# One block's first products moved from plain float32 to three split passes, with reordered first transfers and pinned weight decoding

## The chip, the cores and the metric

The kernel runs on one core of a Trainium2 chip. The metric is device time in microseconds (us) of the whole program: the median of a few executions. A profile of one execution is shown beside it; its span runs from the first instruction to the last, and the execution's own time is a little longer than its span.

## What is computed

Three layers follow each other, all in float32 (shapes in brackets):

```python
# attention: 4 batches, 8 heads, 768 positions, 64 wide; chunks of 32 queries
# see 16 positions to the left, 8 to the right and 8 memory slots
scores = 0.125 * q_c @ k_full.T; a = softmax(scores); out = a @ v_full
x = out as [3072 tokens, 512]
h = x @ w_in                    # [512, 2048]
x = (h * cos(h)) @ w_out        # [2048, 512]
h = max(x @ w1, x @ w2, x @ w3) # each [512, 768]
y = h @ w2o                     # [768, 512]
```

## The kernel before, in words

**Two ways to multiply.** A float32 product on TensorE is made either "plain", one matmul instruction on float32 operands (which the trace shows as two records), or "split": each operand is held as a high part (rounded to the fp32r type by ScalarE, called ACT) and a low part (what the rounding left over, a subtraction on VectorE or GpSimd, called DVE and POOL), and three matmuls, high by high, high by low and low by high, are added up in PSUM. `products` does either, according to how many parts of the moving operand it is given. The low part of a weight must be there before the third matmul of a product.

**Blocks and slots.** The 3072 tokens are 8 blocks of 384 columns, numbered 0 to 7. The first feed-forward layer has 16 feature tiles `f`. A slot is one (block, feature tile): `p1` makes h = w_in[f]ᵀ x (4 products over 512 inputs), `chain` makes g = h cos(h) on ACT and DVE, and `p2`, two slots later (`LOOK`), adds w_out[f]ᵀ g into 4 accumulators (4 products). A tile h lies in one of two PSUM buffers, so the `p1` two slots on needs the `chain` of this one to be done. In block 0 both `p1` and `p2` are plain; from block 1 on both are split. Blocks 6 and 7 are cut into halves of 8 feature tiles, run in the order 6, 7, 6, 7, so that the second layer's weights find room; from block 7's first half (`turn`) on, `p2` comes three slots later (`LOOKB`). When a new block's `p2` begins, the four accumulators must have been copied out by ACT and DVE (L392, L394).

**Attention** of block 0 runs ahead of everything, as a loop of 9 steps (scores at step i, normalizing at i-1, transposing at i-2, values at i-3), each third of it needing its own q, k and v. Later blocks' attention is spread over the slots by tables (`FIRST` for block 0: S scores, E exponentials, N normalizing, T transposing, V values).

**Weights** arrive as 512 KB tiles (`raw`) and must be decoded: a cast makes the top half (`w_top`, on POOL L162 or ACT L160, into one of two `top` buffers in turn), and a shift-and-or on DVE joins both halves (`w_bits`, L177); splitting them is `w_split` (L185 on ACT, then L186 on DVE or POOL). `keysA` lists w_in and w_out tiles alternately, `keysB` the second layer's 24 tiles. `Decode` hands this work out slot by slot, at the places `fill` in `chain`; a scheduler may move these instructions. In block 0 decoded tiles of both kinds are kept plain and split later.

**The second layer** (`b3`, `b4`) runs 48 steps of 36 and 9 matmuls; the last three `p2` stand behind its first `b3`.

All transfers of this kernel are issued by SyncE (SP), in order. `LOADS` is the order of the first ones: q0 is q and k of the first third of block 0, v0 its values, w the next weight tile. By the page's sizes a q is 256 KB (of 1024 bytes), a k 320, a v 384 and a weight tile 512.

Of the kernel before, what the change touches and what calls it, by code (L numbers as in the profile page):

```python
# [32 lines left out]
N = 384  # L33
# [19 lines left out]
FIRST = {0: "S0", 1: "S1", 2: "S2", 3: "E", 5: "N0", 6: "N1 T0", 7: "V0", 9: "T1", 10: "V1", 11: "N2", 12: "T2", 13: "V2"}  # L53
# [6 lines left out]
LOADS = "q0 q1 w q2 v0 v2 w w w w v1 w"  # L60
WARM0, WARM = 11, 2
PRO = (0, 0, 0, 0, 0, 1, 0, 1, 0)
PROL = (1, 2, 0, 2, 2, 3, 0, 3, 2)
PROE = (0, 2, 2, 3, 0, 2, 1, 0, 2)
# [4 lines left out]
RATE, RATEB, AHEADB = 2, 0.75, 4  # L69
# [3 lines left out]
SPLIT0, SPLITS = 5, (1, 1.5)  # L73
# [4 lines left out]
def attn_moe_kernel(ctx, tc, qT, kT, vw, w_in, w_out, w3, w2o, out):  # L78
    nc = tc.nc
    PE, ACT, DVE, POOL, SP = nc.tensor, nc.scalar, nc.vector, nc.gpsimd, nc.sync  # L80

# [73 lines left out]
    def w_top(key, eng):  # L155
        raw = wst[key].rearrange("p c t -> p (c t)").bitcast(BF16).rearrange("p (c t) -> p c t", t=4)[:, :, 2]
        top[key] = tops[len(top) % NTOP]
        o = top[key].bitcast(F16).rearrange("p (c t) -> p c t", t=2)[:, :, 1]
        if eng is ACT:
            ACT.activation(out=o, in_=raw, func=AF.Copy)  # L160
        else:
            eng.tensor_copy(o, raw)  # L162
# [3 lines left out]
    def w_bits(key):  # L166

        z = o = wst[key][:, :, 0]
        if key in numA:
            i, odd = divmod(numA[key], 2)  # L170
            if not odd:
                plain[i] = (wp if i < FA - 1 else tmp["pool"]).tile([128, 2, 512], I32, tag="w", name="wt")
                live[0] += i < FA - 1
# [3 lines left out]
        DVE.scalar_tensor_tensor(o, z, 13, top[key], op0=ALU.logical_shift_right, op1=ALU.bitwise_or)  # L177
        wst[key] = o.bitcast(F32)

    def w_split(key, eng):  # L180
# [4 lines left out]
        ACT.activation(out=w[:, 0, :], in_=c, func=AF.Copy)  # L185
        eng.tensor_tensor(w[:, 1, :], c, w[:, 0, :].bitcast(F32), op=ALU.subtract)  # L186
        n = numA.get(key, -1)
        live[0] -= n % 2 if n < 2 * FA - 1 else 0
# [80 lines left out]
    def a_v(d, ts=(0, 1), pool=None):  # L269
# [3 lines left out]
        if o == 0 and ts[0] == 0:  # L273
            xT[j] = xp.tile([128, 2, 4, N], F32R if j else F32, tag="x", name="x")
# [10 lines left out]
        if j:  # L285
            DVE.tensor_tensor(x[:, 1, :, sl], s[:, :, c0:c1], x[:, 0, :, sl].bitcast(F32), op=ALU.subtract)
# [48 lines left out]
    def p1(j, f, ps):  # L335
# [5 lines left out]
        for k in range(4):  # L341
            products(h, w, k, [x[:, i, k, :] for i in range(2 if j else 1)], k == 0, k == 3)
# [3 lines left out]
    def g_tile(dtype=F32R):  # L346
        p = tmp["pool"] if done[0] else gp
        return p.tile([128, 2, N], dtype, tag="g", name="g", bufs=4 if done[0] else 3)

    def chain(j, f, fill):  # L350
# [135 lines left out]
    class Decode:  # L486


        def __init__(self, keys, exp_eng, lo_eng):
            self.keys, self.exp_eng, self.lo_eng = keys, exp_eng, lo_eng  # L490
            self.nl = self.ne = self.nb = self.ns = 0
# [8 lines left out]
        def room(self):  # L500
            if self.keys is keysB:
                return self.nl - self.ns < AHEADB and live[0] + 3 <= NW
            return self.nl - self.nb < 9 and live[0] + 3 <= NW

        def exp(self, upto):
            while self.ne < min(self.nl, upto, self.nb - len(self.ops) + NTOP):
# [3 lines left out]
        def begin(self, n):  # L510
            keys = self.keys[self.nb:min(self.nb + n, self.nl)]
# [37 lines left out]
    for i in range(2 * DB + 3):  # L549
# [26 lines left out]
    def slot(s):  # L576
# [5 lines left out]
        ready = dec.nb if dec.keys is keysB else 0  # L582
        calm = s < turn or all(slots[s - i][0] == slots[s - i + 1][0] for i in (LOOKB, LOOKB - 1))
        if dec.keys is keysA:
            dec.begin(RATE)
        elif calm:
            dec.begin(max(0, min(2, int(RATEB * (s - turn)) - dec.nb)))
# [137 lines left out]
```

## Time and profile before

| what | us |
|---|---|
| median of three runs | 1080.37 (1078.62 to 1081.43) |
| profiled execution, own time | 1080.69 |
| its span | 1078.8 |
| TensorE (PE) busy | 1059.4 |
| DVE, ACT, POOL busy | 467.4, 434.8, 267.1 |

How to read it: TensorE's busy time is 98% of the span, and in the other 19.4 us it stands still. A matmul counts as busy at whatever clock it is granted, so busy time holds stretches at half clock too. The other engines' idle time costs nothing by itself.

### The profile page before, as it was taken

Reading aid. Unit: us, or ns where it says so; the run is one execution under the profiler, and the core shown is the slowest. Engines: PE = TensorE matmul, PEld = TensorE weight load, DVE = VectorE, ACT = ScalarE, POOL = GpSimd, SP = SyncE. Lnnn points to the kernel's source line nnn. Section 1 sums busy time; section 2 is a strip of 40 time slices with the busy share of each in tenths; the row PEclk is TensorE's granted clock in tenths of the full one; section 3 lists DMA queues with packets and bytes.
Section 4 is the critical chain, followed back from the end, with each engine's and each line's share of the span. In section 5 each row is a group of like instructions: output and inputs, shape, how many; then the busy total and the mean of one; then the engine's idle time right before and its main releaser. Section 6 shows DMA issues by size and latency. Waiting matters only on the chain.

```text
span 1078.8 us, 16695 instructions
## 1 busy us (share of the span) xinstructions
PE 1059.4 (98%) x6861; PEld 978.5 (91%) x6861; DVE 467.4 (43%) x856; ACT 434.8 (40%) x797; POOL 267.1 (25%) x240
## 2 busy tenths in 40 slices
PE   7999999999999999999999999999999999999998
PEld 5565699999999999999999899999999999999997
DVE  5689465555455454544537656222222122312221
ACT  4577455545455454454537657111112121211111
POOL 1356243423233233233313346010101010110000
PEclk8899999999999999999999999999999999999999
DMA  9970121111111111210116525110101020100000
GB/s 319 276 291 17 37 74 52 60 52 52 38 52 52 60 44 38 67 37 16 45 55 196 166 92 167 44 30 30 30 30 30 30 79 10 59 1 31 1 30 30
DMA packets 29837, 76.05 MB, mean 70 GB/s; under 512 B 3392, under 2 KB 8512, under 8 KB 29760
## 3 DMA queue, kind: packets, MB, share of 16 engines
q1 hardware_dynamic: 29760, 74.97, 21.2%
q8 instruction: 54, 0.88, 0.3%
q14 instruction: 23, 0.19, 0.1%
HBM read 60.80 MB, written 14.16 MB: 69 GB/s over the span
## 4 chain that ended last, share of the span: by engine, by line
PE 84%; DMA 5%; DVE 5%; ACT 4%; issue 2%; POOL 0%; SPq 0%; ACTq 0%; DVEq 0%; POOLq 0%
PE h L439 28%; PE h L333 19%; PE acc L333 19%; PE acc L460 9%; PE s L224 3%; PE s L280 2%; PE s L263 2%; PE h L330 1%; DMA v<-in_vw_dram 1%; DMA raw<-in_w2o_dram 1%; PE acc L330 1%; DMA raw<-in_w_dram 1%; DVE w L186 1%; DVE wt L177 1%; DMA raw<-in_w_out_dram 1%
## 5 line engine op out<-in xcount | busy, mean ns | idle before, releaser
L439 PE MATMUL h<-x,w 128*128 128x384 f32 x1728 | 308.5, 335 | 2.2 <-DVE ki L372 2.2
L439 PEld LDWEIGHTS h<-x,w 128*128 128x128 f32 x1728 | 302.0, 188 | 6.5 <-DVE ki L372 2.5
L333 PE MATMUL acc<-g,w 128*128 128x384 f32 x1344 | 257.2, 338 | 2.2 <-ACT x L392 2.2
L333 PE MATMUL h<-x,w 128*128 128x384 f32 x1344 | 255.2, 337 | 0.0
L333 PEld LDWEIGHTS h<-x,w 128*128 128x128 f32 x1344 | 234.8, 188 | 2.9 <-ACT x L284 0.2
L333 PEld LDWEIGHTS acc<-g,w 128*128 128x128 f32 x1344 | 233.0, 188 | 4.1 <-ACT x L392 2.6
L375 POOL TENSOR_TENSOR g<-ki,g 128x384 fp32r<-128x384 f32 x112 | 115.8, 1034 | 274.8 <-ACT g L374 242.4
L367 DVE SCALAR_TENSOR_TENSOR ki<-h,ki 128x384 f32<-128x384 f32 x112 | 62.2, 555 | 144.2 <-ACT ki L365 144.0
L446 DVE TENSOR_TENSOR r<-h,r 128x384 f32<-128x384 f32 x48 | 26.8, 558 | 197.8 <-PE h L439 196.8
L460 PE MATMUL acc<-w,g 128*128 128x512 f32 x432 | 107.3, 393 | 0.0
L421 POOL TENSOR_TENSOR x<-xs,x 128x384 fp32r<-128x384 f32 x31 | 32.6, 1082 | 273.3 <-ACT x L420 273.3
L365 ACT ACTIVATE ki<-h 128x384 int32<-128x384 f32 x112 | 54.2, 484 | 107.0 <-PE h L333 105.6
L370 ACT ACTIVATE ki<-ki,pio 128x384 f32<-128x384 f32 x112 | 68.8, 614 | 68.1 <-DVE ki L368 67.9
L449 ACT ACTIVATE g<-r 128x384 fp32r<-128x384 f32 x48 | 25.1, 523 | 174.5 <-DVE r L447 174.5
L460 PEld LDWEIGHTS acc<-w,g 128*128 128x128 f32 x432 | 80.4, 188 | 14.7
L372 DVE TENSOR_TENSOR ki<-h,ki 128x384 f32<-128x384 f32 x112 | 62.3, 556 | 57.6 <-ACT ki L370 57.2
L374 ACT ACTIVATE g<-ki 128x384 fp32r<-128x384 f32 x112 | 58.5, 522 | 52.7 <-DVE ki L372 52.1
L445 ACT ACTIVATE r<-h 128x384 f32<-128x384 f32 x48 | 23.6, 492 | 130.1 <-PE h L439 130.1
L447 DVE TENSOR_TENSOR r<-h,r 128x384 f32<-128x384 f32 x48 | 26.8, 558 | 66.5 <-PE h L439 66.3
L368 DVE TENSOR_SCALAR ki<-ki 128x384 f32<-128x384 f32 x112 | 51.5, 459 | 3.1
L330 PE MATMUL h<-x,wt 128*128 128x384 f32 x128 | 47.1, 511 | 2.4 <-DVE g L362 1.9
L254 POOL TENSOR_TENSOR sm<-sm,rs 128x768 f32<-128x768 f32 x21 | 30.8, 1471 | 58.4 <-PE h L333 40.8
(80 smaller groups left out, 858.1 us busy)
## 6 DMA issues: line engine op xcount, KB each, us to landing
v<-in_vw_dram SPq DMA_DIRECT2D x24, 384.0 KB, 3.3
raw<-in_w_dram SPq DMA_DIRECT2D x18, 511.8 KB, 3.7
raw<-in_w_in_dram SPq DMA_DIRECT2D x16, 511.8 KB, 9.2
raw<-in_w_out_dram SPq DMA_DIRECT2D x16, 511.8 KB, 9.7
k<-in_kT_dram SPq DMA_DIRECT2D x24, 320.0 KB, 3.7
x2d<-x SPq DMA_DIRECT2D x40, 192.0 KB, 1.9
xs<-x2d SPq DMA_DIRECT2D x20, 384.0 KB, 3.2
q<-in_qT_dram SPq DMA_DIRECT2D x24, 256.0 KB, 2.7
```

Source lines behind the costliest of these rows:

```text
L330: PE.matmul(o, lhsT=w[:, sl], rhs=x[0], start=first, stop=last)
L333: PE.matmul(o, lhsT=w[a][:, sl], rhs=x[b], start=first and n == 0, stop=last and n == 2)
L365: ACT.activation(out=ki, in_=h, func=AF.Copy, scale=INV2PI, bias=0.25)
L367: DVE.scalar_tensor_tensor(c, h, INV2PI, ki, op0=ALU.mult, op1=ALU.subtract)
L368: DVE.tensor_scalar(c, c, -0.75, 0.25, op0=ALU.max, op1=ALU.min)
L370: ACT.activation(out=c, in_=c, func=AF.Sin, scale=2 * math.pi, bias=pio2)
L372: DVE.tensor_tensor(c, h, c, op=ALU.mult)
L374: ACT.activation(out=g[:, 0, :], in_=c, func=AF.Copy)
L375: POOL.tensor_tensor(g[:, 1, :], c, g[:, 0, :].bitcast(F32), op=ALU.subtract)
L421: (DVE if j == 0 and k == 3 else POOL).tensor_tensor(x[:, 1, k, :], t[:, i, :], x[:, 0, k, :].bitcast(F32), op=ALU.subtract)
L439: PE.matmul(h, lhsT=w[a][:, 128 * k:128 * k + 128], rhs=x[:, b, k, :], start=(n == 0), stop=(n == 11))
L460: PE.matmul(o[m], lhsT=g[:, a, 128 * m:128 * m + 128], rhs=w[b], start=(f == 0 and n == 0), stop=(f == FB - 1 and n == 2))
```

## The change

`p1` of block 0 becomes split, so the low half of block 0's x is made too, and each w_in tile is split as soon as it is decoded, always on POOL (`split_in`); only w_out tiles stay plain in block 0, and these are split at half a tile per slot from slot 5 on, at one per slot from slot 16 on (`split_out`, alternately DVE and POOL). v0 and v1 are loaded ahead of all weights. `keep` pins the instructions of decoding and splitting in the order of the program. Block 0's tables place the scores a slot later. For the second layer's weights (`keysB`), up to 6 tiles (4 before) may be loaded and unsplit, a tile is cast only once the slot after its load has come (`there`), decoding starts a slot later, and 3 instead of 2 tiles are taken per step after the slots. `p2` waits one more slot where a block begins, g has 5 buffers instead of 4 there, and one leftover `p2` stands between the second and third product group of the first `b3`.

```diff
-LOADS = "q0 q1 w q2 v0 v2 w w w w v1 w"
+LOADS = "q0 q1 v0 q2 v1 w w v2 w w w w"
...
-RATE, RATEB, AHEADB = 2, 0.75, 4
+RATE, RATEB, AHEADB = 2, 0.75, 6
...
-SPLIT0, SPLITS = 5, (1, 1.5)
+SPLIT0, SPLITS = 5, (0.5, 1)
...
+    keep = tc.keep_in_program_order
...
-        if key in numA:
-            i, odd = divmod(numA[key], 2)
+        if key[0] == "out":
+            i, odd = divmod(key[1], 2)
...
-        DVE.scalar_tensor_tensor(o, z, 13, top[key], op0=ALU.logical_shift_right, op1=ALU.bitwise_or)
+        keep(DVE.scalar_tensor_tensor(o, z, 13, top[key], op0=ALU.logical_shift_right, op1=ALU.bitwise_or))
...
-        if j:
-            DVE.tensor_tensor(x[:, 1, :, sl], s[:, :, c0:c1], x[:, 0, :, sl].bitcast(F32), op=ALU.subtract)
+        DVE.tensor_tensor(x[:, 1, :, sl], s[:, :, c0:c1], x[:, 0, :, sl].bitcast(F32), op=ALU.subtract)
...
-            products(h, w, k, [x[:, i, k, :] for i in range(2 if j else 1)], k == 0, k == 3)
+            products(h, w, k, [x[:, i, k, :] for i in range(2)], k == 0, k == 3)
...
             fill("d0")
+            fill("a0")
             ACT.activation(out=c, in_=c, func=AF.Sin, scale=math.pi)
             ACT.activation(out=c, in_=c, func=AF.Square)
-            fill("a0")
+            fill("a1")
...
         for e in range(3):
+            if e == 2 and n2[0] < total:
+                p2(*slots[n2[0]])
+                n2[0] += 1
...
+        def split_in(self, upto):
+
+            for k in self.keys[self.ni:upto]:
+                if k[0] == "in":
+                    w_split(k, POOL)
+            self.ni = max(self.ni, upto)
+
+        def split_out(self, upto):
+            while self.ns < min(upto, FA):
+                w_split(("out", self.ns), POOL if self.ns % 2 else DVE)
                 self.ns += 1
...
-        ready = dec.nb if dec.keys is keysB else 0
+        ready, dec.there, dec.soon = dec.nb, dec.soon, dec.nl
...
-            while n2[0] <= s - (LOOKB if s >= turn else LOOK):
+            last = s - LOOK
+            if s >= turn:
+                last = s - LOOKB - (slots[s - LOOKB][0] != slots[s - LOOKB - 1][0])
+            while n2[0] <= last:
```

The change shows in the order of instructions at three places. The first is SP's queue at the start of the program, before:

```order
L208 DMA q<-in_qT_dram 128x512
L209 DMA k<-in_kT_dram 128x640
L208 DMA q<-in_qT_dram 128x512
L209 DMA k<-in_kT_dram 128x640
L150 DMA raw<-in_w_in_dram 128x2047
L208 DMA q<-in_qT_dram 128x512
L209 DMA k<-in_kT_dram 128x640
L217 DMA v<-in_vw_dram 96x1024 x2
L150 DMA raw<-in_w_in_dram 128x2047
L150 DMA raw<-in_w_out_dram 128x2047
L150 DMA raw<-in_w_in_dram 128x2047
L150 DMA raw<-in_w_out_dram 128x2047
```

and with the change:

```order
L209 DMA q<-in_qT_dram 128x512
L210 DMA k<-in_kT_dram 128x640
L209 DMA q<-in_qT_dram 128x512
L210 DMA k<-in_kT_dram 128x640
L218 DMA v<-in_vw_dram 96x1024
L209 DMA q<-in_qT_dram 128x512
L210 DMA k<-in_kT_dram 128x640
L218 DMA v<-in_vw_dram 96x1024
L152 DMA raw<-in_w_in_dram 128x2047 x2
L218 DMA v<-in_vw_dram 96x1024
L152 DMA raw<-in_w_out_dram 128x2047
```

v0 has moved ahead of q2, v1 from behind five weight tiles to ahead of all of them, and the first weight tile from behind q1 to behind v1.

The second place is the first product of block 0. On DVE (px is the transposed attention weights, L177 or L179 a decode into raw or wt, L286 a low half of x, L356 the first DVE step of slot 0's chain) stands before:

```order
L318 TENSOR_TENSOR sm<-sm,rs 128x384
L267 COPY px<-s 96x512
L316 TENSOR_SCALAR rs<-rs 128x4
L317 RECIPROCAL rs<-rs 128x4
L177 SCALAR_TENSOR_TENSOR wt<-raw,top_85 128x512
L318 TENSOR_TENSOR sm<-sm,rs 128x384
L177 SCALAR_TENSOR_TENSOR wt<-raw,top_86 128x512
L267 COPY px<-s 96x512
L177 SCALAR_TENSOR_TENSOR wt<-raw,top_85 128x512
L356 SCALAR_TENSOR_TENSOR ki<-h,ki 128x384
```

and with the change:

```order
L316 TENSOR_SCALAR rs<-rs 128x4
L286 TENSOR_TENSOR x<-s,x 128x4x64
L179 SCALAR_TENSOR_TENSOR raw<-raw,top_86 128x512
L317 RECIPROCAL rs<-rs 128x4
L286 TENSOR_TENSOR x<-s,x 128x4x64
L318 TENSOR_TENSOR sm<-sm,rs 128x384
L286 TENSOR_TENSOR x<-s,x 128x4x64
L268 COPY px<-s 96x512
L179 SCALAR_TENSOR_TENSOR wt<-raw,top_85 128x512
L179 SCALAR_TENSOR_TENSOR raw<-raw,top_86 128x512
L286 TENSOR_TENSOR x<-s,x 128x4x64
L179 SCALAR_TENSOR_TENSOR wt<-raw,top_85 128x512
```

The low halves of x have come in between, and two decodes now stand behind the last px copy and ahead of the last low half. On TensorE (s<-k,q are the scores of block 1's first third, L224 or L225) stands before:

```order
L280 MATMUL s<-px,v 64x64 x8
L330 MATMUL h<-x,wt 128x384 x5
L224 MATMUL s<-k,q 64x96 x16
L330 MATMUL h<-x,wt 128x384 x5
L224 MATMUL s<-k,q 64x96 x16
L330 MATMUL h<-x,wt 128x384 x2
L330 MATMUL acc_565<-g,wt 128x384
L330 MATMUL acc_566<-g,wt 128x384
```

and with the change:

```order
L281 MATMUL s<-px,v 64x64 x8
L333 MATMUL h<-x,w 128x384 x24
L225 MATMUL s<-k,q 64x96 x16
L333 MATMUL h<-x,w 128x384 x12
L330 MATMUL acc_593<-g,wt 128x384
L330 MATMUL acc_594<-g,wt 128x384
L330 MATMUL acc_595<-g,wt 128x384
L330 MATMUL acc_596<-g,wt 128x384
L225 MATMUL s<-k,q 64x96 x16
L333 MATMUL h<-x,w 128x384 x12
```

The scores have moved from inside slot 1's products to behind them, so that slot 2's products come right behind the first scores.

The third place is TensorE's order where the second layer begins (h<-x,w at L439 or L443), before:

```order
L333 MATMUL acc_6214<-g,w 128x384 x3
L439 MATMUL h<-x,w 128x384 x36
L333 MATMUL acc_6211<-g,w 128x384 x3
L333 MATMUL acc_6212<-g,w 128x384 x3
L333 MATMUL acc_6213<-g,w 128x384 x3
L333 MATMUL acc_6214<-g,w 128x384 x3
L333 MATMUL acc_6211<-g,w 128x384 x3
```

and with the change:

```order
L333 MATMUL acc_6371<-g,w 128x384 x3
L443 MATMUL h<-x,w 128x384 x24
L333 MATMUL acc_6368<-g,w 128x384 x3
L333 MATMUL acc_6369<-g,w 128x384 x3
L333 MATMUL acc_6370<-g,w 128x384 x3
L333 MATMUL acc_6371<-g,w 128x384 x3
L443 MATMUL h<-x,w 128x384 x12
L333 MATMUL acc_6368<-g,w 128x384 x3
```

One leftover `p2` has moved from behind the third group of 12 matmuls to ahead of it.

## Rows read from the trace of the kernel before

**Rows 1.** The page: busy time; granted TensorE clock in 40 slices, in tenths.

```profile
PE 1059.4 (98%) x6861; PEld 978.5 (91%) x6861; DVE 467.4 (43%) x856; ACT 434.8 (40%) x797; POOL 267.1 (25%) x240
...
PEclk8899999999999999999999999999999999999999
```

**Rows 2.** Chain that ended last, 0 to 135 us: start, us, what.

```profile
30.63 5.71 PE h L330 x10
...
114.37 2.58 PE h L330 x8
...
124.69 2.09 PE h L333 x12
```

**Rows 3.** TensorE's waits: line, releaser, us in all, times, longest.

```profile
PE h L330 <- DVE g L362: 1.9, 2, 1.6
```

**Rows 4.** Timeline 14 to 40 us: start, us, engine, instruction, [idle before].

```profile
14.51 0.77 POOL L162 CAST top<-raw 128x512 f16<-128x512 bf16 x1 [5.53 <-DMA raw<-in_w_in_dram]
...
22.45 1.12 PE L280 MATMUL s<-px,v 96*64 96x64 f32 x16 [4.63 <-DMA v<-in_vw_dram]
...
30.19 0.38 ACT L284 ACTIVATE x<-s 128x256 f32<-128x256 f32 x1 [2.62 <-PE s L280]
...
37.33 1.09 DVE L236 TENSOR_TENSOR sm<-s,maskb 128x384 f32<-128x384 f32 x2
...
38.45 0.95 DVE L241 TENSOR_REDUCE mx<-sm 128x8 f32<-128x768 f32 x1
...
39.32 0.54 DVE L362 SCALAR_TENSOR_TENSOR g<-ki,h 128x384 f32<-128x384 f32 x1
```

**Rows 5.** Four stretches: us, busy us (instructions) by engine, clock, DMA share, GB/s.

```profile
22.45:30.63 8.18, 6.83 (x75) 5.28 (x75) 2.45 (x4) 2.12 (x5) 1.52 (x2) 0.50 1.04 338
30.63:36.34 5.71, 5.71 (x12) 2.97 (x14) 0.09 (x1) 0.59 (x2) 0.00 (x0) 0.61 1.04 266
106.00:108.00 2.00, 0.39 (x2) 0.30 (x2) 0.61 (x2) 1.97 (x5) 0.38 (x1) 1.00 0.00 0
612.00:614.00 2.00, 2.00 (x8) 2.00 (x7) 1.30 (x2) 1.96 (x4) 1.38 (x2) 0.50 0.81 290
```

**Rows 6.** Groups by form, 40 to 92 us: count, busy us, mean ns, idle.

```profile
L177 DVE SCALAR_TENSOR_TENSOR wt<-raw,top 128x512 int32<-128x512 int32 x28 | 26.6, 978 | 2.0 <-POOL top L162 1.3 <-ACT top L160 0.7
...
L162 POOL CAST top<-raw 128x512 f16<-128x512 bf16 x13 | 11.6, 894 | 12.0 <-DVE wt L177 11.2 <-DMA raw<-in_w_out_dram 0.8
...
L186 POOL TENSOR_TENSOR w<-wt,w 128x512 fp32r<-128x512 f32 x6 | 8.7, 1445 | 7.7 <-ACT w L185 7.7
...
L246 ACT ACT_TABLE_LOAD x2 | 2.6, 1283 | 0.0
```

**Rows 7.** Timeline 92 to 108 us: DVE and POOL making low halves.

```profile
92.65 4.29 DVE L186 TENSOR_TENSOR w<-wt,w 128x512 fp32r<-128x512 f32 x3
...
93.22 4.87 POOL L186 TENSOR_TENSOR w<-wt,w 128x512 fp32r<-128x512 f32 x3 [0.18 <-ACT w L185]
...
107.62 1.27 POOL L186 TENSOR_TENSOR w<-wt,w 128x512 fp32r<-128x512 f32 x1 [2.72 <-DVE g L362]
```

**Rows 8.** Timeline 608 to 671 us: the two late waits of TensorE.

```profile
608.49 0.78 ACT L160 ACTIVATE top<-raw 128x512 f16<-128x512 bf16 x1 [0.88 <-DMA raw<-in_w2o_dram]
...
609.91 0.86 ACT L392 ACTIVATE x<-acc 128x384 f32<-128x384 f32 x2
...
610.44 3.21 PE L333 MATMUL acc<-g,w 128*128 128x384 f32 x12 [2.24 <-ACT x L392]
...
616.43 2.24 PE L333 MATMUL acc<-g,w 128*128 128x384 f32 x12
...
670.81 2.37 PE L439 MATMUL h<-x,w 128*128 128x384 f32 x12 [2.21 <-DVE ki L372]
```

**Rows 9.** The page's transfers of w1 to w3, to landing; and the chain.

```profile
raw<-in_w_dram SPq DMA_DIRECT2D x18, 511.8 KB, 3.7
...
693.98 6.26 PE h L439 x36
```

More of the change, by code (lines that the diff above doesn't have):

```diff
@@ L159, in w_top @@
         if eng is ACT:
-            ACT.activation(out=o, in_=raw, func=AF.Copy)
+            keep(ACT.activation(out=o, in_=raw, func=AF.Copy))
         else:
-            eng.tensor_copy(o, raw)
+            keep(eng.tensor_copy(o, raw))
     plain = {}
@@ L184, in w_split @@
         assert live[0] <= NW
[L185 to L188, printed above, removed]
+        keep(ACT.activation(out=w[:, 0, :], in_=c, func=AF.Copy))
+        keep(eng.tensor_tensor(w[:, 1, :], c, w[:, 0, :].bitcast(F32), op=ALU.subtract))
+        live[0] -= key[0] != "out" or key[1] % 2 and key[1] < FA - 1
         DST[key[0]][key[1]] = (w[:, 0, :], w[:, 1, :])
@@ L273, in a_v @@
         if o == 0 and ts[0] == 0:
-            xT[j] = xp.tile([128, 2, 4, N], F32R if j else F32, tag="x", name="x")
+            xT[j] = xp.tile([128, 2, 4, N], F32R, tag="x", name="x")
         x = xT[j]
@@ L347, in g_tile @@
         p = tmp["pool"] if done[0] else gp
-        return p.tile([128, 2, N], dtype, tag="g", name="g", bufs=4 if done[0] else 3)
+        return p.tile([128, 2, N], dtype, tag="g", name="g", bufs=5 if done[0] else 3)
     def chain(j, f, fill):
@@ L501, in room @@
             if self.keys is keysB:
-                return self.nl - self.ns < AHEADB and live[0] + 3 <= NW
+                return self.nl - self.ns < AHEADB and live[0] + 5 <= NW
             return self.nl - self.nb < 9 and live[0] + 3 <= NW
         def exp(self, upto):
-            while self.ne < min(self.nl, upto, self.nb - len(self.ops) + NTOP):
+            while self.ne < min(self.there if self.keys is keysB else self.nl, upto, self.nb - len(self.ops) + NTOP):
                 w_top(self.keys[self.ne], self.exp_eng(self.ne))
@@ L510, in begin @@
         def begin(self, n):
-            keys = self.keys[self.nb:min(self.nb + n, self.nl)]
+            keys = self.keys[self.nb:min(self.nb + n, self.there if self.keys is keysB else self.nl)]
             self.nb += len(keys)
@@ L580, in slot @@
         base = DB * (j + 1)
-        ready = dec.nb if dec.keys is keysB else 0
-        calm = s < turn or all(slots[s - i][0] == slots[s - i + 1][0] for i in (LOOKB, LOOKB - 1))
+        ready, dec.there, dec.soon = dec.nb, dec.soon, dec.nl
+        calm = s < turn or s < total - 3 and all(slots[s - i][0] == slots[s - i + 1][0] for i in (LOOKB, LOOKB - 1))
         if dec.keys is keysA:
@@ L595, in fill @@
                 if where == "a0":
-                    dec.split(min(parts, len(keysA)))
+                    dec.split_in(ready)
+                elif where == "a1":
+                    dec.split_out(parts)
             elif where in ("a0", "a1"):
@@ L600, in fill @@
                 dec.bits(1)
-            elif where == "z" and calm:
-                dec.bits()
+            elif where == "z":
+                if calm:
+                    dec.bits()
+                    dec.exp(dec.nb + 2)
                 dec.load()
-                dec.exp(dec.nb + 2)
         p1(j, f, ps)
@@ L658, in attn_moe_kernel @@
         if n == 0:
-            for s in range(n2[0], total):
-                p2(*slots[s])
+            while n2[0] < total:
+                p2(*slots[n2[0]])
+                n2[0] += 1
         if n >= LOOK:
```

25 lines of the change are left out of this document (14 added, 11 removed).

## The prediction

> **What bounds the kernel now.** I read the page first. TensorE is busy for 98% of the span, and the clock row reads 9 (90% or more) but for slices at the start, where it reads 8 [rows 1]: so only three things are worth time, fewer TensorE cycles, less waiting of TensorE, and its clock.
>
> Fewer cycles: the chain of waits gives the price of the two kinds of product. In block 0's steady part four plain products (8 records) take 2.58 us, and block 1's first four split products (12 matmuls) 2.09 [rows 2].
>
> Waiting: TensorE's list of waits and the timeline name four places. It waits 4.63 us for v1, which sits behind five weight tiles in SP's queue [rows 4]; 1.9 us in two waits for the last step of a chain in block 0 (L362) [rows 3]; 2.24 us at 610 for ACT to empty an accumulator (L392), which ACT does late; and 2.21 us at 668 for a PSUM tile of the last chain [rows 8]. 1.3 us at the start and some 5 us at the end are of no concern here.
>
> Clock: the windows view shows the level. After the v1 wait it is 0.50 (1.2 GHz) all the way to the first product, and 0.61 on average over the first ten records, which take 5.71 us [rows 2, 5]. After the wait at 610 it reads 0.50 too, but after the one of about 1.6 us that ends at 107.66 the window reads 1.00 [rows 3, 5].
>
> **The change part by part.** I sum against the profiled execution's own time, 1080.69, which is 0.3 above the median.
>
> *Passes.* 16 `p1` of block 0 become split: 16 x (2.58 - 2.09) = **-7.8 us** at full clock. All block 0's other TensorE work stays. A lower bound is 0, if another engine then sets the pace (a rival below); more is excluded, as nothing else in block 0 loses cycles.
>
> *Prologue.* Six transfers then stand ahead of the last v instead of the weights. In today's trace the second weight tile, which closes the first 3.60 MB in the queue, has landed by 14.51 [rows 4]; with the change the same first 3.60 MB (by the sizes in the section on the kernel) hold three q and k, v0, v1 and two weight tiles, so v1, at 2.56 MB, is there well before TensorE asks for it at 22.45 - 4.63 = 17.82. From 22.45 to the first product at 30.63 are 8.18 us, of which TensorE is busy 6.83 at half clock [rows 2, 5]; at full clock that is 3.4 less, so the product could start at 17.82 + 8.18 - 3.4 = 22.6. New work stands ahead of it on DVE: six low halves of x, for which the nearest row is ACT's copy of the same half block, 0.38 [rows 4], and four decodes; their mean of 0.98 [rows 6] holds many that ran beside busy POOL work, and I take 0.7, since POOL has little to do yet. That is 6 x 0.38 + 4 x 0.7 = 5.1 us. DVE has room for about 1.5 of it while TensorE works; the last decode also waits for a POOL cast that queues behind the first weight's low half (0.9 and 1.27 [rows 6, 7]), which runs beside the px copies. I take 3.6 as exposed: start at 26.2, a gain of **-4.4 us**. Bounds: 22.6 (-8.0) to 30.6 (0). The first five plain products took 5.71 us and at 2.58 per four would take 3.2: with no long wait ahead of them the clock stays, **-2.5 us** (bounds -2.5 to 0).
>
> *A wait that comes in return.* Block 1's first scores move behind slot 1's products. DVE then has two additions (1.09) and a maximum (0.95) between them and slot 0's g (0.54) [rows 4], and slot 2's `p1` needs slot 0's PSUM tile. Today the scores run early, in the middle of slot 1. TensorE now reaches slot 2 as the scores end, the first addition begins half way through them, and so 0.55 + 0.95 + 0.54 = 2.0 us of DVE stand between. Slot 3 inherits a little: ACT has an exponential between the two chains with a table load on either side (1.28 each [rows 6]; in block 0 there are seven loads now, five before), and I put 0.8. Together **+2.8 us**; 0 if DVE gets to g earlier, 5 if the later two thirds cost as much.
>
> The table load is a place to weigh a rule. Rows 6 give 1.283 us for one, and in the timeline the ACTIVATE behind it starts at once. The Trainium skill ("ScalarE: Activation LUTs", What ACT_TABLE_LOAD costs) counts 2.66 us for a switch, a drain included; by that the two new ones would hold ACT 2.8 us longer, and the sum would be about 17 instead of 20 us. The trace does not agree, and no term uses it.
>
> *The rest of block 0.* The two waits of 1.9 us stand where the low halves of weights pile up on DVE and POOL: three on each take 4.29 and 4.87 us there, against 1.27 for a lone one on POOL [rows 3, 7]. Pinned and spread, none piles up: **-1.9 us** (0 to -1.9). ACT's extra roundings, 16 in block 0 instead of about half as many, and POOL's extra subtractions lie beside TensorE's 4.67 us a slot (2.58 + 2.09). If that cover is gone, the second rival tells.
>
> *The turn.* At 610 the new block's `p2` comes a slot later, so one more `p1` (2.09) lies over ACT's copy, and ACT is no longer held by casts of tiles that have not landed (0.88 at 608). The wait of 2.24 goes, and with it the half clock after it: from 610.44 to 616.43 are 5.99 us for two groups of 2.09, so 1.8 more. **-4.0 us** (bounds: 0 to -4.0). At 668, a `p2` of 2.09 fills the 2.21: **-2.1 us** (0 to -2.2) [rows 8].
>
> *Second layer.* Ten or so weight tiles are decoded in its first steps that were decoded before it. The 36 matmuls of a step alone take 6.3 us and the tiles fall due from the fifth step on, after 25 us or more, while a transfer lands in 3.7 us [rows 9] and up to six are in flight: **0**, with its price in the third rival.
>
> Sum: -7.8 - 4.4 - 2.5 + 2.8 - 1.9 - 4.0 - 2.1 = **-19.9**, so 1080.7 - 19.9 = 1060.8.
>
> **The rivals.**
>
> *First: the clock falls at the start.* Between 17.8 and 26 TensorE has only 3.4 us of this work in 8.4, with gaps that I estimate at 1 us each, and then the 2.0 us of the new wait. For it: after 2.24 us at 610 the clock fell [rows 5, 8]. Against it: after 1.6 us at 106 it did not. Half clock over the first two slots would give back the 2.5 and about 2 more: 1065.
>
> *Second: DVE and POOL set block 0's pace.* All w_in low halves go to POOL, beside DVE's decodes. For it: a decode takes 0.98 on average between 40 and 92 us, and POOL's low half 1.45 there against 1.27 alone [rows 6, 7]. Against it: in the pile-up three of each, made in 4.87 us, overlapped in part, and DVE loses about half of its own low halves. Counting a slot from rows 4 and 6, DVE has two decodes (2.0), the chain's two steps (2 x 0.54) and attention (an estimate: three times 1.09 + 0.95, and as much again for what follows, over 16 slots, 0.8): 3.9 us in a slot of 4.67, which is near. If the slot stayed at today's 2 x 2.58 = 5.16 from slot 4 on, 12 x 0.49 = 5.9 would be lost: 1066.7. At the worst POOL's 2.7 (a cast 0.9, a low half 1.45, a quarter of one more for w_out) would come wholly on top of DVE's 3.9, a slot would take 6.6, and 12 x 1.4 = 17 more would be lost: 1084. Most of that is excluded, since today's POOL has 1.6 a slot beside the same DVE work and TensorE waits for neither until 99 us. The Trainium skill ("GPSIMD Engine Reference", the specification table) says that POOL's way to SBUF is shared with VectorE and contended by instructions with two SBUF inputs, as decodes and low halves are; the lengthened rows agree that it is shared, the pile-up that it is not one at a time.
>
> *Third, on the other side: late weights of the second layer.* Were the ten late tiles fetched and converted one by one, each would take 3.7 + 0.9 (cast) + 1.0 (decode) + 1.45 (low half) = 7.0 us, 70 in all, against some 25 until they fall due: 45 us of waiting, 1106. It decides where fewer than three tiles are on the way at once; with six there is no wait. For it: ACT waits for landings today, 0.88 us of one at 608 [rows 8]. Against it: SP has nothing else to do then.
>
> *Fourth: better than said*, with the prologue at its bound and no new wait: 1055.
>
> **How the numbers follow.** Forecast (1057 to 1063) 0.45; first rival (1062 to 1067) 0.17; second (1063 to 1076) 0.2; fourth (1053 to 1057) 0.1; third (over 1084) 0.04; gains that cancel for reasons I don't see (1077 to 1084) 0.04. From 1054 to 1069 hold 0.8 of it. A measurement of this kernel tells about 0.3% (3.2 us) from no change; so faster 0.93, same 0.03, slower 0.04.
>
> **What would show it.** Right: TensorE's wait for v gone and its first split product near 26; a wait of about 2 us for L363 near 31; windows of 20 to 40 us at clock 1.00; no waits from 50 to 130; block 0's slots 0.49 shorter; no wait for L393 near 590; the first `b3` without a gap. Wrong: the windows at 0.50 near 30; many short waits of TensorE for DVE or POOL between 50 and 110; waits for raw tiles beyond 650. The prediction fails most easily in block 0, where one engine more in the pace undoes the passes.

## The result, and the profile after

The changed kernel takes 1064.99 us (median of 4 runs, 1064.47 to 1066.60); the kernel before took 1079.49 beside it (4 runs). The ratio is 0.9872, 95% interval 0.9843 to 0.9902: faster by 1.3%. The profiled execution's own time is 1064.75, its span 1062.5. The forecast was 1060.8, with 1054 to 1069 as its range; 1065 is where the first rival stood.

First the page after, its first group and its clock row, against [rows 1]:

```profile
PE 1048.6 (99%) x6925; PEld 986.2 (93%) x6925; DVE 460.0 (43%) x854; ACT 437.7 (41%) x799; POOL 281.0 (26%) x248
...
PEclk9899999999999999999999999999999999999999
```

Then TensorE's timeline around the first products (start, us, engine, instruction, idle before), which answers to [rows 2, 4]:

```profile
25.69 0.45 PE L333 MATMUL h<-x,w 128*128 128x384 f32 x1 [0.48 <-ACT x L285]
27.85 5.62 PE L333 MATMUL h<-x,w 128*128 128x384 f32 x23 [1.72 <-DVE x L286]
33.41 1.54 PE L225 MATMUL s<-k,q 64*64 64x96 f32 x32
37.05 3.75 PE L333 MATMUL h<-x,w 128*128 128x384 f32 x12 [2.11 <-DVE g L363]
...
40.60 2.96 PE L330 MATMUL acc<-g,wt 128*128 128x384 f32 x8
43.49 1.54 PE L225 MATMUL s<-k,q 64*64 64x96 f32 x32
45.49 2.35 PE L333 MATMUL h<-x,w 128*128 128x384 f32 x12 [0.46 <-DVE g L363]
47.68 2.74 PE L330 MATMUL acc<-g,wt 128*128 128x384 f32 x8
```

The wait of 4.63 us for v1 is gone. In its place stand 1.72 for the last low half of x and 2.11 for slot 0's g. Twelve split matmuls take 3.75 us at 37.05 and 2.35 at 45.49: the first group has less clock, as these windows show (columns as in rows 5):

```profile
26.00:28.00 2.00, 0.28 (x2) 0.15 (x1) 1.80 (x2) 0.00 (x0) 2.00 (x3) 0.85 1.03 390
28.00:30.00 2.00, 2.00 (x7) 2.00 (x8) 1.14 (x1) 0.00 (x0) 0.76 (x2) 0.50 1.09 271
...
36.00:38.00 2.00, 0.95 (x4) 0.95 (x5) 2.00 (x4) 1.02 (x1) 1.75 (x2) 0.91 1.04 246
38.00:40.00 2.00, 2.00 (x8) 2.00 (x8) 2.00 (x3) 1.53 (x2) 0.09 (x1) 0.50 1.01 356
```

The clock falls to 0.50 (1.2 GHz) twice, each time after a stretch in which TensorE was mostly idle. From 50 us on nothing of this is left, and the late stretch of [rows 8] has no wait either:

```profile
70.00:90.00 20.00, 20.00 (x143) 15.37 (x142) 12.54 (x21) 14.18 (x28) 11.46 (x9) 1.00 0.27 93
...
600.00:660.00 60.00, 60.00 (x349) 60.00 (x348) 35.86 (x56) 35.06 (x67) 28.33 (x26) 1.00 0.36 123
```

In slots without attention, two groups (p1 and p2) take 4.66 us from one `p1` to the next, as 2.09 + 2.58 said:

```profile
105.00 2.54 PE L333 MATMUL h<-x,w 128*128 128x384 f32 x12
...
109.66 2.54 PE L333 MATMUL h<-x,w 128*128 128x384 f32 x12
```

The same mark in both programs tells where the gain came. At the turn (the first pair of `p1`, 24 matmuls of L333) and at the second layer's first `b4`, the timelines of TensorE before read

```profile
562.28 4.32 PE L333 MATMUL h<-x,w 128*128 128x384 f32 x24
...
691.74 2.24 PE L460 MATMUL acc<-w,g 128*128 128x512 f32 x9
```

and after

```profile
552.70 4.32 PE L333 MATMUL h<-x,w 128*128 128x384 f32 x24
...
675.42 2.24 PE L464 MATMUL acc<-w,g 128*128 128x512 f32 x9
```

That is 9.6 us by the turn, where the terms up to there made 13.8, and 16.3 by the first `b4`, so 6.7 from the turn on, where the terms made 6.1.

### The profile page after: what moved, and what is told of

Read it like the earlier page. It is cut to its first block, busy times and chain, and to the rows that moved or that the text cites. A ratio compares the mean times of both kernels' runs of the same rounds, so it can differ in the third digit from the quotient of the medians.

```text
span 1062.5 us, 16809 instructions
## 1 busy us (share of the span) xinstructions
PE 1048.6 (99%) x6925; PEld 986.2 (93%) x6925; DVE 460.0 (43%) x854; ACT 437.7 (41%) x799; POOL 281.0 (26%) x248
## 4 chain that ended last, share of the span: by engine, by line
PE 98%; ACT 1%; DVE 1%; issue 0%; DMA 0%; POOL 0%; ACTq 0%
PE h L443 28%; PE h L333 26%; PE acc L333 22%; PE acc L464 9%; PE acc L330 4%; PE s L225 3%; PE s L281 2%; PE s L264 2%; PE warm L560 1%; DMA out_dram<-ost 0%; ACT L371 0%; ACT L247 0%; ACT L306 0%; POOL top L164 0%; ACT sm L306 0%
## 5 line engine op out<-in xcount | busy, mean ns | idle before, releaser
L443 PE MATMUL h<-x,w 128*128 128x384 f32 x1728 | 308.4, 335 | 0.0
L443 PEld LDWEIGHTS h<-x,w 128*128 128x128 f32 x1728 | 302.0, 188 | 4.0
L333 PE MATMUL h<-x,w 128*128 128x384 f32 x1536 | 297.2, 341 | 4.8 <-DVE g L363 2.6
L333 PEld LDWEIGHTS h<-x,w 128*128 128x128 f32 x1536 | 269.6, 189 | 12.1 <-DVE g L363 3.0
L333 PE MATMUL acc<-g,w 128*128 128x384 f32 x1344 | 256.5, 337 | 0.0
L333 PEld LDWEIGHTS acc<-g,w 128*128 128x128 f32 x1344 | 232.6, 188 | 1.6 <-DVE x L397 0.4
L375 ACT ACTIVATE g<-ki 128x384 fp32r<-128x384 f32 x112 | 58.7, 524 | 55.4 <-DVE ki L373 54.7
L188 POOL TENSOR_TENSOR w<-raw,w 128x512 fp32r<-128x512 f32 x28 | 41.6, 1486 | 67.8 <-ACT w L187 65.2
L369 DVE TENSOR_SCALAR ki<-ki 128x384 f32<-128x384 f32 x112 | 48.3, 431 | 3.0
```

Source lines behind the costliest of these rows:

```text
L188: keep(eng.tensor_tensor(w[:, 1, :], c, w[:, 0, :].bitcast(F32), op=ALU.subtract))
L333: PE.matmul(o, lhsT=w[a][:, sl], rhs=x[b], start=first and n == 0, stop=last and n == 2)
L369: DVE.tensor_scalar(c, c, -0.75, 0.25, op0=ALU.max, op1=ALU.min)
L375: ACT.activation(out=g[:, 0, :], in_=c, func=AF.Copy)
L443: PE.matmul(h, lhsT=w[a][:, 128 * k:128 * k + 128], rhs=x[:, b, k, :], start=(n == 0), stop=(n == 11))
```

## The experiments

Each kernel was timed beside the kernel before on the same chip; the ratio is to that one. Single profiled executions differ by some 2 us in the first 25 us with no cause in the edits: in e6 and e7, whose instructions are the same there, transfers land later, the very first scores wait 1.8 and 2.0 us for k between 8 and 13 us, in the changed kernel not at all, and the first product comes at 26.98 and 27.17 instead of 25.69. Where that matters below, the stretch from the first product to the mark at the turn is compared (527.0 us in the changed kernel).

| label | edit | us, median (range) | ratio, 95% |
|---|---|---|---|
| (the change) | | 1064.99 (1064.5 to 1066.6) | 0.9872 (0.9843 to 0.9902) |
| e1_scores_early | first scores a slot earlier again | 1072.14 (1069.6 to 1072.8) | 0.9917 (0.9897 to 0.9936) |
| e2_decodes_back | first decodes earlier, none last | 1072.07 (1069.3 to 1073.4) | 0.9915 (0.9896 to 0.9934) |
| e3_late | before, with the late parts only | 1077.34 (1074.6 to 1078.8) | 0.9963 (0.9949 to 0.9977) |
| e4_loads | before, with the new transfer order only | 1079.75 (1075.1 to 1080.9) | 0.9985 (0.9972 to 0.9999) |
| e5_loads_back | change, old transfer order | 1069.73 (1067.5 to 1070.8) | 0.9901 (0.9882 to 0.9920) |
| e6_two_passes | change, block 0's third pass left out | 1060.42 (1057.5 to 1063.2) | 0.9814 (0.9790 to 0.9838) |
| e7_pinned_chain | change, block 0's g and block 1's additions pinned | 1062.83 (1062.5 to 1063.7) | 0.9839 (0.9817 to 0.9861) |
| e8_warm | change, 14 small matmuls in the gaps | 1065.67 (1064.0 to 1068.3) | 0.9869 (0.9848 to 0.9890) |
| e9_pinned_warm | e7 and e8 together | 1061.94 (1061.3 to 1064.3) | 0.9818 (0.9796 to 0.9840) |
| e10_unpinned | change, nothing pinned | 1088.40 (1085.4 to 1092.0) | 1.0059 (1.0038 to 1.0080) |
| e11_x_first | e9, low halves of x ahead of decodes | 1063.86 (1060.6 to 1065.3) | 0.9831 (0.9808 to 0.9855) |
| e12_late_v | e11, two v later, two q and k earlier | 1061.20 (1060.5 to 1063.0) | 0.9821 (0.9807 to 0.9834) |

### The transfers' order: e4, e5

```diff
-LOADS = "q0 q1 w q2 v0 v2 w w w w v1 w"
+LOADS = "q0 q1 v0 q2 v1 w w v2 w w w w"
```

e4 makes this one edit in the kernel before, e5 undoes it in the changed kernel.

> The kernel before with only the order of the first transfers changed (v0 and v1 ahead of five of the weight tiles that stood ahead of v1). Theory (the wait of 4.63 us for v1 and the half clock behind it are due to the order alone): the wait falls below 0.5 and 5 to 7 us are won, 1072.5 to 1074.5. Rival (the weight tiles, now later, are waited for instead, since the casts of the start stand in a fixed place on POOL ahead of other work): less than 2.5 us, 1077 or more, with TensorE waiting for DVE or POOL work that follows a cast.

e4's theory fell. TensorE's timeline in it:

```profile
24.47 3.49 PE L330 MATMUL h<-x,wt 128*128 128x384 f32 x10 [0.47 <-ACT x L284]
31.86 2.82 PE L224 MATMUL s<-k,q 64*64 64x96 f32 x32 [3.90 <-DMA k<-in_kT_dram]
34.62 5.00 PE L330 MATMUL h<-x,wt 128*128 128x384 f32 x10
```

The first product comes at 24.47 instead of 30.63 and takes 3.49 instead of 5.71 [rows 2], 8.4 us together, more than the prediction's two terms (4.4 and 2.5, with low halves of x to make, which e4 does not). Then the first scores wait 3.90 us for k, and what follows runs at half clock: 2.82 for scores that take 1.54 in the changed kernel (at 33.41), and 5.00 for ten more records of products. Of the 8.4 us, 0.15% of the time (1.6 us) is left. The rival was right that something else would be waited for, but named the wrong transfer.

> The changed kernel with the first transfers in the order of before (v1 behind five weight tiles); all else as changed. Theory (the transfer engines are busy without a break for the first 45 us or so, so an order is worth what the first product needed gets earlier by: in the changed kernel nothing but v1 is late in that order, the scores having moved away from k): a wait of TensorE for v of 4 to 5 us comes back, and the kernel is 4 to 7 us slower than the change, 1069 to 1072. Rival (the order is worth as little here as in the kernel before, since what is saved at v1 is waited for elsewhere): within 1.5 us of the change, 1064 to 1066.5.

In the changed kernel, where TensorE comes to these scores only at 33.4 us, and not at 28.0 as in e4, the same order does pay: undoing it costs 4.7 us by the medians, within the theory, and brings the wait back, 3.30 us and not the 4 to 5 expected, with the clock at 0.50 from 24 to 36. By the ratios it is 0.29%, and the two intervals overlap a little, so the size is not settled:

```profile
22.87 1.12 PE L281 MATMUL s<-px,v 96*64 96x64 f32 x16 [3.30 <-DMA v<-in_vw_dram]
```

Why an order can merely move a wait is in the windows of the changed kernel (the last two columns are the busy share of the 16 transfer engines and GB/s): they are full until 50 us.

```profile
20.00:30.00 10.00, 6.02 (x78) 4.76 (x77) 7.76 (x14) 3.18 (x7) 6.30 (x6) 0.87 1.04 375
...
40.00:50.00 10.00, 9.54 (x64) 7.01 (x62) 6.38 (x14) 7.59 (x14) 5.69 (x6) 0.95 1.03 402
50.00:60.00 10.00, 10.00 (x71) 7.91 (x70) 9.41 (x13) 8.85 (x12) 7.12 (x6) 1.00 0.66 228
```

That k is there in time is not the moved scores' doing, as the theory had it: e1 below, with the old table, comes to them at 32.47 and waits nothing for k. What is later is TensorE itself, with split matmuls at half clock ahead of the scores (24, in e1 19); in e11, where all 24 run at full clock, it comes at 30.23 and waits 2.81 us.

### The moved scores: e1, e7

e1 puts the old table back into the changed kernel; e7 keeps the new one and pins the last step of block 0's chains (g) and the additions of block 1's scores in program order. e1's edit:

```diff
-FIRST = {1: "S0", 2: "S1", 3: "S2", 4: "E", 6: "N0", 7: "N1 T0", 8: "V0", ...
+FIRST = {0: "S0", 1: "S1", 2: "S2", 3: "E", 5: "N0", 6: "N1 T0", 7: "V0", ...
```

> The changed kernel with block 1's first scores where they stood before (S0 in slot 0, S1 in slot 1, S2 in slot 2, and what follows one slot earlier). Theory (the moved scores put two additions and a maximum of DVE ahead of slot 0's g, and the clock falls behind that wait): the wait of 2.11 us for DVE's L363 that ends at 37.05 goes or falls below 0.8, the window 36 to 40 reads above 0.9, and the kernel is 2 to 4 us faster than the change, 1061 to 1063. Rival (DVE owes that work in the first slots wherever the scores stand, so another wait of about the same length takes its place): within 1 us of the change, 1064 to 1066, with a wait of 1.5 us or more for DVE between 28 and 45.

The wait for slot 0's g did fall to 1.03 and the windows from 36 to 40 read 1.00, but the kernel is slower by 0.45% (0.9917 against 0.9872), which neither expected. POOL's timeline in e1, and what TensorE waits for:

```profile
41.61 1.47 POOL L255 TENSOR_TENSOR sm<-sm,rs 128x768 f32<-128x768 f32 x1 [4.21 <-ACT ki L355]
43.04 1.74 POOL L188 TENSOR_TENSOR w<-raw,w 128x512 fp32r<-128x512 f32 x1
...
44.83 2.03 PE L333 MATMUL h<-x,w 128*128 128x384 f32 x10 [0.95 <-POOL w L188]
...
55.28 1.47 POOL L255 TENSOR_TENSOR sm<-sm,rs 128x768 f32<-128x768 f32 x1 [0.41 <-DVE rs L254]
56.70 1.74 POOL L188 TENSOR_TENSOR w<-raw,w 128x512 fp32r<-128x512 f32 x1
...
58.50 1.95 PE L333 MATMUL h<-x,w 128*128 128x384 f32 x6 [2.28 <-POOL w L188]
```

Attention's normalization on POOL now stands ahead of the low half that the next slot needs. A third wait, 2.14 us for another g (L363), ends at 67.36, behind a decode of 1.91 that waited 1.77 for a POOL cast. The moved scores are not only a cost: they keep POOL free while the first weights come through.

> The changed kernel with the last step of block 0's chains (L363) and the additions of block 1's scores (L237) kept in program order, so that slot 0's g stands ahead of the first scores' additions and maximum on DVE. Theory (those 2.0 us of DVE make TensorE wait 2.11 us for slot 0's g, and the half clock of 38 to 40 follows that wait): the wait falls below 0.5, the windows of 36 to 42 read 0.9 or more, 2 to 4 us faster than the change, 1061 to 1063. Rival (slot 0's g is late because of ACT's table loads and the transfers behind the weights; what is later now, the scores' exponential and normalization, is waited for instead): within 1 us, 1064 to 1066, or slower.

Met in the main: the wait is 1.03 instead of 2.11 (not below 0.5), the windows from 36 on read 1.00, and the median is 1062.83, inside 1061 to 1063. From the first product to the turn it takes 2.4 us less than the changed kernel. By the ratios the gain is 0.33%, but the intervals overlap, so its size is not settled.

```profile
37.12 2.35 PE L333 MATMUL h<-x,w 128*128 128x384 f32 x12 [1.03 <-DVE g L363]
```

What is left of the wait is ACT's: DVE stands idle 2.27 us ahead of this g, for L360, the last ACT step of the chain. In this the rival, which named ACT, had a part.

### The clock and the last low half of x: e8, e2, e9, e11

> The changed kernel with 14 small bfloat16 matmuls more (128x384, about 0.25 us each, result unused) in TensorE's gaps between 22 and 28. Theory (the clock falls at 28 because TensorE has little work from 22 to 28, 6.0 us in 10): the windows of 28 to 32 read above 0.9, the first 23 products take about 4.1 us instead of 5.6, 1 to 2 us faster than the change, 1063 to 1064. Rival (the small matmuls do not hold the clock, or lie in the way of the transposes and products of the start): the windows still show 0.50, or the first product comes later by as much, no gain, 1065 or more.

The first half of the theory is shown, the gain is not. With 14 small matmuls in the gaps the windows from 20 to 36 read 1.00 (one of them below), and the 23 matmuls take 4.26 us instead of 5.62.

```profile
28.00:30.00 2.00, 1.60 (x9) 1.61 (x10) 1.48 (x3) 0.00 (x0) 1.31 (x2) 1.00 1.07 279
```

In its timeline of TensorE the next wait has stayed:

```profile
28.39 4.26 PE L333 MATMUL h<-x,w 128*128 128x384 f32 x23 [1.02 <-DVE x L286]
...
36.23 3.39 PE L333 MATMUL h<-x,w 128*128 128x384 f32 x12 [2.11 <-DVE g L363]
```

The time does not move (0.9869): the first product comes 1.2 us later (26.90), the wait of 2.11 is still there and half clock behind it too (3.39 us for the twelve matmuls), so that slot 2 starts 0.8 us earlier than in the changed kernel, and the mark at the turn, 552.26, is 0.4 earlier.

> Both of the two edits before together: slot 0's g pinned ahead of the scores' additions, and 14 small matmuls in TensorE's gaps between 22 and 28. Theory (the wait for slot 0's g and the half clock over the first products are two losses, each hidden by the other as long as only one is taken away: what the small matmuls win was spent in the wait behind the additions): the windows of 26 to 42 all read above 0.9, the waits for L363 stay below 1.2 in all, and 1 to 1.5 us are won over the pinned kernel, 1061 to 1062. Rival (the first slots are paced by the transfers and by the conversions behind them, so an earlier first product only waits longer for weights): within 0.6 us of the pinned kernel, 1062.3 to 1063.4, with more waits for POOL's low halves (L188).

```diff
+    LATE = (6, 8)
...
+        if i > 2 * DB:
+            for _ in range(LATE[i - 2 * DB - 1]):
+                PE.matmul(wl[:, :384], lhsT=zb[:96, :128], rhs=..., start=True, stop=True)
...
-            DVE.scalar_tensor_tensor(g[:, 0, :], c, 0.5, h, ...)
+            keep(DVE.scalar_tensor_tensor(g[:, 0, :], c, 0.5, h, ...))
```

Both losses away: no wait for L363 at all, clock 1.00 in every window from 20 to 50, and the mark at the turn at 549.43, 3.3 us ahead of the changed kernel's (their first scores start within 0.01 us of each other):

```profile
35.03 2.35 PE L333 MATMUL h<-x,w 128*128 128x384 f32 x12
```

The median is 1061.94, as expected; over e7 it is 0.9 us, which the intervals do not resolve.

> The changed kernel with the first three weight tiles decoded one step earlier and none in the last three steps of the start (PRO 0 0 0 1 1 1 0 0 0), so that no decode stands ahead of the last low halves of x. Theory (the decode stretched to 1.73 us ahead of the last low half makes TensorE wait 1.72 us, and the half clock over the first products follows that wait): the wait for DVE's L286 falls below 0.6, the windows of 28 to 32 read above 0.9, 2 to 3.5 us faster than the change, 1061.5 to 1063. Rival (the clock falls because TensorE has little to do all through the start, not because of that one wait): the wait goes, but the clock is still at 0.50 somewhere in the first 4 us of products, and at most 1.5 us are won, 1063.5 or more.

The theory fell, and the rival held: the wait for L286 is down to 0.59, the clock is at 0.50 all the same, and nothing is won. That e2 is even slower, by 0.43% (0.9915 against 0.9872), neither expected. With the early decodes one more weight tile is asked for ahead of k, and TensorE waits there, then for weights, of which the start now decodes three instead of five:

```profile
36.13 1.54 PE L225 MATMUL s<-k,q 64*64 64x96 f32 x32 [2.61 <-DMA k<-in_kT_dram]
...
49.73 2.03 PE L333 MATMUL h<-x,w 128*128 128x384 f32 x10 [1.76 <-POOL w L188]
```

On the clock: it read 0.50 at 28 to 30 although no wait between 15 us and the first products (at 27.23) was longer than 0.73: it was not that one wait.

> The kernel with both edits (pinned g, small matmuls) in which the last low halves of x are pinned too, and the decode that stood ahead of the last one comes behind it. Theory (TensorE's wait of 1.0 to 1.7 us for L286 is that decode, stretched to 1.73): the wait falls below 0.4, the first product's rest starts at 26.5 to 27.2 instead of 27.9 to 28.9, 0.7 to 1.5 us won over the kernel with both edits, about 1060 to 1061. Rival (the weight of slot 2 is decoded later and split later, so slot 2 waits for POOL's L188 by as much): within 0.5 us of it, or slower.

The wait for L286 is gone, and all 24 first matmuls run from 25.73 to 30.23; then the scores wait 2.81 us for k. No gain over e9: the transfers again.

> The kernel with pinned g, small matmuls and pinned low halves of x, in which q and k of the first two scores are fetched one step earlier and their two v (0.77 MB, needed from slot 8 on) only at slot 4. Theory (the transfer engines are full until 50 us, so each of the first slots waits for whatever is last in the queue; 0.77 MB fewer ahead are about 2 us at the 400 GB/s of that stretch): the waits of 2.81 us for k and 0.65 us for L188 fall below 1 us together, 1.5 to 3 us faster than the kernel without it, 1060.5 to 1062.5. Rival (k is late because of when it is asked for, and the order only hands the wait on): the sum of the waits for k and for L188 between 25 and 60 stays above 2 us, within 1 us of the kernel without it, 1063 to 1065.

The wait for k is gone and 0.79 us for L188 are left, as the theory said, and the median is 1061.20. But a wait of 2.46 for slot 0's g has come, now behind ACT's part of the chain (DVE is idle 1.64 us before it, for ACT's L360), and against e11 the intervals overlap. e9 and e12 are the fastest kernels of the study that make every pass (e6 leaves one out), and lie below both kernels: e12's interval, 0.9807 to 0.9834, is clear of the change's.

### The pinning and the late parts: e10, e3

```diff
-    keep = tc.keep_in_program_order
+    keep = lambda i: i
```

> The changed kernel without the pinning: the casts, decodes and splittings may be put in any order on their engines. Theory (the pinning is what keeps low halves from piling up at 92 to 107 and casts out of ACT's way at the turn): waits of 1.5 to 2 us between 50 and 130 and of 1 to 2 us near 600 come back, 2 to 5 us slower than the change, 1067 to 1070. Rival (the plan that splits each w_in at once and spreads w_out spreads the work by itself): within 1 us of the change, 1064 to 1066.

The theory had the sign; the size is several times larger, 23 us by the medians and 1.9% by the ratios, which makes the changed kernel slower than before. The timeline of the start in e10 (POOL, DVE, TensorE):

```profile
13.35 0.76 POOL L164 CAST top<-raw 128x512 f16<-128x512 bf16 x1 [11.15 <-DMA raw<-in_w_in_dram]
...
14.14 0.69 DVE L179 SCALAR_TENSOR_TENSOR raw<-raw,top 128x512 int32<-128x512 int32 x1 [5.13 <-POOL top L164]
...
17.37 1.06 PE L264 MATMUL s<-ident,sm 128*96 128x128 f32 x4 [4.22 <-DVE sm L318]
...
36.02 0.45 PE L333 MATMUL h<-x,w 128*128 128x384 f32 x1 [0.48 <-ACT x L285]
```

The first decode has slipped ahead of attention's normalization. It waits for a cast, the cast for a transfer, and DVE stands for 5.13 us; behind it TensorE waits 4.22 and then goes on at half clock, and the first product comes at 36.02 instead of 25.69. The Trainium skill ("PSUM — Partial Sum Buffer", Engine vs sequencer instructions) says that the queues of these engines are strictly first in, first out; the row agrees. Later TensorE waits 3.93 us for L363 (until 74.93, half clock behind it), 1.14 (until 111.80) and, at the turn, 0.93 for L393. By the marks 17.8 us are lost up to the turn and 3.1 behind it.

e3 makes only the late parts, in the kernel before:

> The kernel before with only the change's late parts: second products a slot later at a block boundary, second products between the second layer's groups, two more transfers ahead there, five g buffers, casts only of tiles that were asked for a slot earlier. Theory (these parts end the waits of 2.24 and 2.21 us and the half clock behind the first, whatever block 0 does): 6 to 7 us faster than before, 1072.5 to 1074, no wait of TensorE over 1 us from 540 on. Rival (part of what the late stretch won in the change comes from block 0's weights being split sooner, which gives ACT and DVE room there): 3 us or less, 1076.5 or more.

The theory fell: 0.37% (0.23 to 0.51), so some 4 us by the ratios, and 3.1 by the medians. The size is near the rival's 3, but not for its reason. The fill at the second layer takes the wait of 2.21 away (0.41 for a g, L375, is left at 674.40), and at the turn 1.65 us of waits stay. ACT and TensorE in e3:

```profile
610.62 0.77 ACT L160 ACTIVATE top<-raw 128x512 f16<-128x512 bf16 x1 [0.70 <-DMA raw<-in_w2o_dram]
611.26 0.46 ACT L392 ACTIVATE x<-acc 128x384 f32<-128x384 f32 x1
...
611.77 0.79 PE L333 MATMUL acc<-g,w 128*128 128x384 f32 x3 [1.31 <-ACT x L392]
```

A cast of a tile still on its way stands ahead of the accumulator's copy. The rule that casts only landed tiles places it later in the program, but without the pin it does not stay there; e10's wait for L393 is of the same kind. With the pin both copies stand together at 595.68 and nobody waits. The marks bear this out: from the turn to the first `b4` e3 wins 3.0 us, and e10 loses 3.1, together 6.1 of the change's 6.7. No run adds the pin alone to e3.

### What sets block 0's pace: e6

> The changed kernel in which block 0's first products leave out the third pass (weights' low half by x's high half), so 64 matmuls of about 0.173 us fewer; the conversions stay. Theory (TensorE alone sets block 0's pace from slot 4 on): the 11.1 us that the matmuls took are won but for the first slots, 9 to 11 us, 1054 to 1056, with at most 2 us of new waits from 50 on. Rival (DVE and POOL are next to the pace, since DVE is busy 9.4 of 10 us between 50 and 70): the slots do not get shorter than DVE's and POOL's work allows, 5 us or less are won, 1060 or more, with new waits for DVE or POOL between 50 and 110.

Not settled by the time: 4.6 us by the medians, as the rival said, 6.9 by the spans of the profiled executions and 8.2 from the first product to the turn, of 11.1. The windows show where the rest stayed:

```profile
50.00:70.00 20.00, 16.63 (x107) 11.43 (x105) 15.83 (x25) 16.50 (x27) 14.27 (x12) 1.00 0.85 328
70.00:90.00 20.00, 19.54 (x123) 14.37 (x123) 14.28 (x22) 13.77 (x28) 11.69 (x10) 1.00 0.27 93
```

From 71 us on TensorE sets the pace (20.00 us busy from 90 to 110). Up to there a shorter slot runs into the work of the other engines: three waits for L363 after 50, 2.9 us in all. Ahead of the longest, 1.31, DVE makes a decode of 1.76 for which it waited 1.44 for a POOL cast; ahead of the first, 0.84, DVE itself waits for ACT's L360.

## Why the prediction was right, and where not

Most of what was to show it right came: no wait for v, the first split product at 25.69, a wait of 2.11 for L363 (though it ends at 37, not near 31), no wait from 50 on. But one sign of being wrong came too, the windows at 0.50 near 30, where the sum had 1.00 throughout. The time lies in the range because the first rival's price was inside it. That it lies on that rival's 1065 is in part chance: of the rival's 4.5 us the clock cost 3.0, and a late second matmul the rest.

**Passes** (-7.8). Right: slots of 4.66 us instead of 5.16, no wait from 50 to 140. The second rival (DVE and POOL set the pace) did not come about, but e6 and e1 show that between 40 and 70 us it is the next bound. (POOL's 1.6 us a slot in that rival is too low: the casts and low halves of [rows 6], 11.6 + 8.7 us in 52, are 2.0 per slot of 5.16, attention not counted.)

**Prologue** (-4.4 and -2.5). The cause named, v1 behind five weight tiles, was only half of it: e4 removes it and wins 1.6 us. (Seven transfers stand ahead of v1 in the new order, not six; the 2.56 MB are right.) The step that fell short is "I take 0.7, since POOL has little to do yet". After, the decode ahead of the last low half of x took 1.73, beside POOL's low half of w_in:

```profile
25.62 1.29 POOL L188 TENSOR_TENSOR w<-raw,w 128x512 fp32r<-128x512 f32 x1
...
25.73 1.73 DVE L179 SCALAR_TENSOR_TENSOR raw<-raw,top 128x512 int32<-128x512 int32 x1 [0.66 <-POOL top L164]
27.39 0.41 DVE L286 TENSOR_TENSOR x<-s,x 128x256 fp32r<-128x256 f32 x1
```

So the second matmul stands at 27.85, not at 26.4 (26.2 and one matmul): 1.45 late. 0.8 of that was there from the start (first scores at 5.99 against 5.21; the 11 first matmuls took 3.83 to 4.88 in kernels of the study that begin alike, so this need not be the change's; e1, whose first scores stand at 5.16, has its first product 0.75 earlier).

**The clock** was a rival, and should have been in the sum. The first products give back 5.62 - 4.26 = 1.4, and slot 2's two groups 3.75 + 2.96 - 2.35 - 2.74 = 1.6. With 1.45 and less 0.35 (slot 3's wait is 0.46, not 0.8) that makes 4.1 of the 4.2 us that are missing at the turn. Each of these is read from rows, not won back one by one: e8 took the first of these away and won 0.4 us at the turn, because the next wait stood behind it.

**The new wait** (+2.0). Right to 0.1 us (2.11), by the mechanism named; the scores end at 34.95, and DVE goes on:

```profile
34.33 1.22 DVE L237 TENSOR_TENSOR sm<-s,maskb 128x384 f32<-128x384 f32 x2 [1.24 <-PE s L225]
35.58 0.95 DVE L242 TENSOR_REDUCE mx<-sm 128x8 f32<-128x768 f32 x1
36.45 0.55 DVE L363 SCALAR_TENSOR_TENSOR g<-ki,h 128x384 f32<-128x384 f32 x1
```

e7 removes half of it; the other half is ACT's part of the chain, which this term did not have. With the old table the wait is 1.03, behind the same additions (e1), so the move itself costs about one us. Its price alone was the wrong account, though: the move also keeps POOL free (e1).

**Waits at 99 and 107, the turn, the fill** (-1.9, -4.0, -2.1). All these waits went; the late parts made 6.7. But much of it is the pinning, which the sum priced inside the -1.9 and which e10 shows to be worth some 20 us within this plan, 3.1 of them behind the turn. The third rival (late weights of the second layer) did not occur.

## What to carry to other kernels

Where the transfer engines are full, a new order can merely move a wait (e4); it pays where what is put back is asked for later (e5, e12). Work that waits for a transfer must not be free to slip ahead of work on the path, on an engine that takes its queue in order: pin it. Of two losses in a row on the same path (a half clock, then a wait), taking away the first alone may not be seen in the time (e8), because the second takes up what it gave.

## What the runs showed of the hardware

A decode on DVE (two SBUF operands) and POOL's work on SBUF overlapped by no more than about 0.1 us. Between 20 and 130 us of the changed kernel a decode that began during a low half, a subtraction or a normalization on POOL ended 0.54 to 0.56 us after it (10 places); a low half that began during a decode ended 1.15 to 1.19 us after that (11 places). Alone they take 0.68 and 1.27:

```profile
58.50 1.47 POOL L255 TENSOR_TENSOR sm<-sm,rs 128x768 f32<-128x768 f32 x1 [0.41 <-DVE rs L254]
...
58.69 1.83 DVE L179 SCALAR_TENSOR_TENSOR wt<-raw,top 128x512 int32<-128x512 int32 x1
```

58.50 + 1.47 + 0.55 is 58.69 + 1.83. The Trainium skill ("SBUF — State Buffer", SBUF: two separate sides) calls it an exclusive lock on a shared pair of ports, held for the whole instruction. The rows agree but for that 0.1 us, and the prediction was wrong to read the pile-up [rows 7] as a partial overlap: its three low halves on each engine took from 92.65 to 98.09, 5.44 us, and one after the other they would take 3 x 0.68 + 3 x 1.27 = 5.85. Such costs add up across the two engines.
